# Products of ones ahead of the first load, the last weight splits behind a table, factors behind a copy, two chunks ahead of the weights

## The chip, the cores and the metric

The kernel runs on one core of a Trainium2 chip (trn2). The metric is the device time of one execution in microseconds. The core has TensorE (PE), VectorE (DVE), ScalarE (ACT), GpSimd (POOL) and SyncE (SP); in this kernel SP issues the plain loads and POOL the indirect scatters and stores.

## What is computed

Attention over channels for four batches, then a mixture of eight experts, of which each token uses one:

```python
qn = q / (np.linalg.norm(q, axis=1, keepdims=True) + 1e-06)
kn = k / (np.linalg.norm(k, axis=1, keepdims=True) + 1e-06)
s = kn.transpose(0, 2, 1) @ qn / tau            # B=4, N=5056, C=256
a = softmax(s, axis=-1)
x = (v @ a).reshape(B * N, C)                   # 20224 tokens
logits = x @ w_gate                             # E=8 experts
expert_idx = np.argmax(logits, axis=1)
gate_w = softmax(logits)[token, expert_idx]
out = gate_w * (relu(x @ w1[e]) @ w2[e])        # F=1024, e = expert_idx of the token
```

## The kernel before

**Attention.** `attention(b, ...)` is a generator and each `yield` is a point where other work may be given out. A batch has 20 chunks of scores: a chunk loads 512 KB of q and k (L203), squares it on ScalarE (L213, L215), adds the squares on VectorE (L216) and multiplies k by q on TensorE, either as it is (a native chunk, L223, f32) or split into a high and a low part (L186, L187, then L227 and L228). Batch 0 is native throughout; of batch 1, chunk 0 and those from 14 on are split. Then come the norms, the softmax and the attention matrix `a_x` (L240 to L326), and then ten groups of 512 values: products with `a_x` (L363 in batch 0, L366 later), the choice of the expert and the row's slot (L376 to L440), and four indirect scatters of the rows into `xs`, sorted by expert (L443). A group is two `yield`s.

**Weights.** `weights()` is a generator too. For each of eight experts it loads four 512 KB pieces (L120, tied behind batch 0's last load of scores), finds their scale by a gram product (L158), its diagonal (L162) and a sum over partitions (L123, L84, L85), and then splits each of the two f32 halves into two f16 parts: a cast on ScalarE (L112) and a subtraction on VectorE (L113). The sixteen results fill the tile `W`; most raw halves are loaded into places of `W` that are free by then, the last two into buffers of the tag `hl`, of which there are two. A half's split is given out while the next expert is loaded; only those of the last expert taken, number 4, are left for the end, where `both` and `fe` (the factors that undo the scales) are made as well.

**Table and blocks.** `table(s)` works out on VectorE, from the counts of tokens so far, which blocks of 256 sorted rows are full; table 0 rests on the first six groups of batch 0 and yields five blocks. `block_load` (called by `look`) waits on SP for the table's entry, then loads a block's rows, transposed (`xT`, L584), and the rows' gate weight and number (`mt`, L586). `block` copies eight pieces of its expert's weights out of `W` at an address from a register (L600, five buffers), multiplies (L612), applies the relu and splits (L619, L620), multiplies by the second weights (L634), scales by the factor `fac` (L640, from `mt` and `fe`; L645) and stores by an indirect DMA (L647).

**Order.** The code gives instructions out in the order in which it calls the generators, and the framework's scheduler then puts each engine's list in order: what comes first in the code has precedence, but where its list has a gap by the scheduler's own reckoning, ready work from further down is put in. On the chip every engine and every queue then runs its list strictly in order. `tc.issue_after(x)` ties what is made under it behind `x` in the list of its engine; it adds no wait.

The opening runs so: the first two chunks of batch 0; constants; then a loop over steps 2 to 32, which takes one step of `first` (batch 0) each; at step 20, when batch 0's 20 chunks are out and this step gives out norms and softmax, it also takes 14 steps of `weights`, then 2 at each step; from step 23 on also one chunk of `second` (batch 1), ten in all. Then what is left of the weights, table 0, the first two blocks' loads, the rest of batch 0, and the loop over blocks, into which the other batches are interleaved by a planner (`want`, `s_at`), with `START` standing for the ten chunks given out before.

## Time and profile before

| | us |
|---|---|
| median of 3 runs | 1187.32 (1187.19 to 1194.84) |
| profiled execution | 1184.51 |
| its span, first to last instruction | 1182.7 |
| TensorE busy | 1151.0 |
| VectorE busy | 906.6 |
| ScalarE busy | 645.5 |
| GpSimd busy | 388.7 |

The profile is one execution. The span is a little shorter than the execution's time, as something lies around the instructions. Busy times are sums of records; an f32 product leaves two records. Times on the timeline count from the start of the span, and where several instructions of one line follow each other a row gives their start, their joint length and their count. The granted clock is a share of TensorE's upper level, 2.4 GHz; 0.50 is the lower, 1.2 GHz.

### The profile page before, as it was taken

The page shows a single profiled execution, that of the slowest core. Times are in us where ns is not written, and L with a number is a line of the kernel's source. Part 1 is how long each engine was busy: PE and PEld are TensorE (multiplying, and loading weights), DVE is VectorE, ACT ScalarE, POOL GpSimd, SP SyncE. Part 2 cuts the span into 40 slices and gives each one's busy share as a digit, 9 for nine tenths or more (in the row PEclk, how much of TensorE's full clock was granted, in tenths as well). Part 3 has the DMA queues.
Part 4 walks back from the last instruction along what each step waited for, and adds up shares of the span by engine and source line. Part 5 has one row for each costly group of instructions (what it writes and reads, how often), then busy time and mean ns, then how long its engine had stood idle before and what let it go on. Part 6 is the DMA issues. An engine that isn't in the chain of part 4 may idle for free.

```text
span 1182.7 us, 28145 instructions
## 1 busy us (share of the span) xinstructions
PE 1151.0 (97%) x10212; PEld 1022.5 (86%) x10212; DVE 906.6 (77%) x2384; ACT 645.5 (55%) x1362; POOL 388.7 (33%) x366
## 2 busy tenths in 40 slices
PE   8898899999999999999999999999999999999998
PEld 7777688999888889999888889999888888889897
DVE  6789898888987777777888777777865566656986
ACT  6399864887655546666655536666432323332332
POOL 0047651466512223544622112445421111111111
PEclk9889999999999999999999999999999999999999
DMA  8976874545564433453355434433242122121221
GB/s 328 408 293 246 215 195 120 144 117 144 141 152 125 126 81 100 115 129 100 101 157 129 122 91 105 120 100 79 72 106 55 46 55 55 46 51 39 40 55 31
DMA packets 147870, 145.91 MB, mean 123 GB/s; under 512 B 115980, under 2 KB 117393, under 8 KB 147728
## 3 DMA queue, kind: packets, MB, share of 16 engines
q1 hardware_dynamic: 132336, 102.48, 33.0%
q0 software_dynamic: 15392, 41.60, 9.8%
q8 instruction: 81, 1.33, 0.5%
q14 instruction: 61, 0.50, 0.1%
HBM read 80.03 MB, written 43.29 MB: 104 GB/s over the span
## 4 chain that ended last, share of the span: by engine, by line
PE 54%; issue 25%; DVE 7%; DMA 5%; POOL 4%; ACT 3%; SPq 1%; POOLq 0%; DVEq 0%; ACTq 0%
PE y L634 19%; PE hp L612 19%; PE px L366 7%; POOL out L647 4%; PE sp L227 3%; PE sp L223 2%; DMA W<-in_w 2%; PE sp L228 2%; DVE W L113 1%; DVE ht L620 1%; DVE rows L385 1%; DVE hl L187 1%; DMA xs<-rows,r_si 1%; PE px L363 1%; ACT xjunk L370 1%
## 5 line engine op out<-in xcount | busy, mean ns | idle before, releaser
L612 PE MATMUL hp<-xT,wp 128*128 128x256 f16 (+1 forms) x4320 | 449.4, 262 | 0.7 <-DVE ht L620 0.5
L634 PE MATMUL y<-wp,ht 128*128 128x256 f16 x3888 | 446.6, 273 | 0.5 <-DVE ht L620 0.5
L612 PEld LDWEIGHTS <-wp 128*128 128x128 f16 x4320 | 381.8, 98 | 45.6 <-issue 3.4
L634 PEld LDWEIGHTS <-ht 128*128 128x128 f16 x3888 | 373.3, 98 | 52.5 <-issue 3.6
L647 POOL DMA_INDIRECT out<-o,mt x162 | 181.1, 1118 | 628.5 <-ACT o L645 599.5
L600 DVE COPY wp<-W 128x1024 f16 x720 | 298.5, 428 | 92.2 <-PE y L634 65.0
L619 ACT ACTIVATE ht<-hp 128x512 f16<-128x512 f32 x324 | 191.6, 594 | 160.1 <-PE hp L612 112.7
L620 DVE SCALAR_TENSOR_TENSOR ht<-hp,ht 128x512 f16<-128x512 f32 x324 | 219.5, 685 | 22.5 <-ACT ht L619 20.9
L443 POOL DMA_INDIRECT xs<-rows,r_si x160 | 187.4, 1172 | 121.6 <-issue 41.6
L645 ACT ACTIVATE o<-y,b_fac 128x256 f32<-128x256 f32 x162 | 68.7, 469 | 191.7 <-PE y L634 181.2
L366 PE MATMUL px<-a_h,hl 128*128 128x264 f32 x480 | 98.0, 296 | 0.0
L384 ACT ACTIVATE rows<-xg,x_sc 128x256 f16<-128x256 f32 x160 | 69.1, 497 | 31.6 <-DVE r_ex L417 22.4
L187 DVE TENSOR_TENSOR hl<-raw,hl 128x1024 fp32r<-128x1024 f32 x47 | 57.5, 1224 | 30.4 <-ACT hl L186 30.4
L366 PEld LDWEIGHTS px<-a_h,hl 128*128 128x128 f32 x480 | 78.9, 188 | 1.4 <-issue 0.6
L186 ACT CAST hl<-raw 128x1024 fp32r<-128x1024 f32 x47 | 49.0, 1044 | 46.5 <-PE sp L228 39.8
L227 PE MATMUL sp<-hl 128*128 128x512 f32 x188 | 72.8, 420 | 1.1 <-DVE hl L187 1.1
L223 PE MATMUL sp<-raw 128*128 128x256 f32 x264 | 64.2, 400 | 5.9 <-DMA raw<-in_qk 5.9
L215 ACT ACTIVATE raw<-raw 128x1024 f32<-128x1024 f32 x44 | 46.6, 1059 | 42.7 <-DVE hl L187 41.8
L385 DVE SCALAR_TENSOR_TENSOR rows<-xg,x_sc,rows 128x256 f16<-128x256 f32 x160 | 69.6, 479 | 0.2 <-ACT rows L384 0.2
L370 ACT ACTIVATE xjunk<-xg 128x256 bf16<-128x256 f32 x160 | 66.6, 416 | 3.3
L366 PE MATMUL px<-a_l,hl 128*128 128x264 f32 x240 | 68.2, 284 | 0.0
L223 PEld LDWEIGHTS sp<-raw 128*128 128x128 f32 x264 | 52.1, 201 | 13.7 <-DMA raw<-in_qk 6.2
(142 smaller groups left out, 928.8 us busy)
## 6 DMA issues: line engine op xcount, KB each, us to landing
raw<-in_qk SPq DMA_DIRECT2D x80, 512.0 KB, 4.3
vraw<-in_vT SPq DMA_DIRECT2D x34, 512.0 KB, 4.2
W<-in_w SPq DMA_DIRECT2D x28, 512.0 KB, 9.1
v<-in_vT SPq DMA_DIRECT2D x12, 256.0 KB, 8.8
out<-o,mt POOLq DMA_INDIRECT x162
xs<-rows,r_si POOLq DMA_INDIRECT x160
wraw<-in_w SPq DMA_DIRECT2D x4, 512.0 KB, 5.2
xT<-xs SPq DMA_TRANSPOSE x90, 3.3
```

The costliest lines, as they stand in the source:

```text
L223: pe.matmul(sp[c][:, 0, :], raw[:, j, kc0 : kc0 + P], raw[:, j, 0:C], start=first, stop=last)
L227: pe.matmul(sp[c], hl[:, 0, j, kc0 : kc0 + P], hl[:, :, j, 0:C], start=first, stop=False)
L366: pe.matmul(px, hl[:, vh, c, ts], ah[:, c, :], start=(n == 0), stop=(n == 5))
L370: act.activation(junk, xg[:, t, 0:C], AF.Square, accum_out=ss[:, t : t + 1])
L385: vec.scalar_tensor_tensor(out=r16[:, t, C : 2 * C], in0=x, scalar=sc[:, t : t + 1], in1=r16[:, t, 0:C], op0=ALU.mult, op1=ALU.subtract,)
L443: ins = pool.indirect_dma_start(out=xs[:, :], out_offset=bass.IndirectOffsetOnAxis(ap=si[:n, t : t + 1], axis=0), in_=rows[:n, t, :], in_o ...
L600: vec.tensor_copy(out=t, in_=Wf[:, ds(e * 8192 + n * 1024, 1024)])
L612: pe.matmul(hp[:, f % nf, :], wp[:, dc, wh, (f % 2) * P : (f % 2 + 1) * P], xT[:, 2 * xh + dc, :], start=(n == 0), stop=(n == 5),)
L619: act.activation(ht[:, 0], hp, AF.Relu)
L620: vec.scalar_tensor_tensor(out=ht[:, 1], in0=hp, scalar=0.0, in1=ht[:, 0], op0=ALU.max, op1=ALU.subtract)
L634: pe.matmul(ys[j], hts[f // nf][:, hh, f % nf, j * P : (j + 1) * P], wp[:, f % 2, wh, :], start=(f == 0 and n == 0), stop=(f == 7 and n == 2),
L647: pool.indirect_dma_start(out=out[:, :], out_offset=bass.IndirectOffsetOnAxis(ap=mt.bitcast(I32)[:, j, 1:2], axis=0), in_=o, in_offset=Non ...
```

## The change

Four things. (1) `ones16` is made ahead of everything, and thirty 128 x 128 x 128 products of it into an unused bank stand first in TensorE's list. (2) At step 20 two chunks of batch 1 are given out in front of the weights; the loop takes its ten as before, so twelve are out when it ends, and `START` stays. (3) `weights()` yields once more behind its last scale, the loop stops there (33 steps are `4 * E + 1`), and the last two splits, `both` and `fe` are given out behind table 0 and the first two blocks' loads. (4) A block's factor is tied behind the copy of its seventh piece of weights.

```diff
--- before.py
+++ after.py
@@ -165,7 +165,9 @@
                 )
             summed.append((e, gram, dsum, list(zip(pair, raws))))
             yield
+
         scale(*summed.pop())
+        yield
         while ready:
             split_one()
         both = tiny.tile([P, E], F32, name="w_both", bufs=1)
@@ -595,9 +597,11 @@
             skip_runtime_bounds_check_because=WHY,
         )
 
+        copied = [None]
+
         def piece(n):
             t = work.tile([P, 1024], F16, tag="wp", name="wp", bufs=WP)
-            vec.tensor_copy(out=t, in_=Wf[:, ds(e * 8192 + n * 1024, 1024)])
+            copied[0] = vec.tensor_copy(out=t, in_=Wf[:, ds(e * 8192 + n * 1024, 1024)]).ins
             return t
 
         hts = []
@@ -637,7 +641,9 @@
                     )
                     n += 1
             if f == 4:
-                vec.tensor_scalar(out=fac, in0=mt[:, :, 0], scalar1=fe[:, ds(e, 1)], scalar2=None, op0=ALU.mult)
+
+                with tc.issue_after(copied[0]):
+                    vec.tensor_scalar(out=fac, in0=mt[:, :, 0], scalar1=fe[:, ds(e, 1)], scalar2=None, op0=ALU.mult)
             if f % 2 == 1 and f < 7:
                 yield
         for j in range(nj):
@@ -658,15 +664,20 @@
 
     def take(gen, n):
         for _ in range(n):
-            if next(gen, StopIteration) is StopIteration:
-                return False
-        return True
+            next(gen, None)
+        return n
 
     nch = NP // P // 2
     normal = [(ps_a, "acc")] * 2
     wts = weights()
     first = attention(0, [False] * nch, False, [(ps_y, "y0"), (ps_y, "y1")])
     second = attention(1, [i == 0 or i >= NATIVE for i in range(nch)], True, normal)
+
+    ones16 = one.tile([P, P], F16, name="ones16")
+    vec.memset(ones16, 1.0)
+    idle = ps_t.tile([P, 512], F32, tag="tp", name="idle")
+    for _ in range(30):
+        pe.matmul(idle[:, 0:P], ones16, ones16, start=True, stop=True)
     take(first, 2)
 
 
@@ -679,8 +690,6 @@
     tri32 = work.tile([P, P], F32, tag="junk", name="tri32", bufs=1)
     sync.dma_start(out=tri32, in_=kc[:, K_TRI:K_N])
     vec.tensor_copy(out=tri, in_=tri32)
-    ones16 = one.tile([P, P], F16, name="ones16")
-    vec.memset(ones16, 1.0)
     ones = one.tile([P, P], F32, name="ones")
     vec.memset(ones, 1.0)
     wg = kt[:, K_WG : K_WG + 2 * E].rearrange("p (c e) -> p c e", c=2)
@@ -694,12 +703,14 @@
     vec.memset(done, 0.0)
     fe = one.tile([P, E], F32, name="fe")
 
+    weighed = 0
     for step in range(2, nch + 1 + 2 * CUT):
         take(first, 1)
-        take(wts, 0 if step < nch else 14 if step == nch else 2)
+        if step == nch:
+            take(second, 2)
+        weighed += take(wts, 0 if step < nch else min(14 if step == nch else 2, 4 * E + 1 - weighed))
         if step > nch + 2:
             take(second, 1)
-    run(wts)
     tables = {0: table(0)}
 
     def streams():
@@ -727,6 +738,7 @@
     side, s_at = streams(), 0.0
     look(0)
     look(1)
+    run(wts)
     run(first)
     for n, (s, i) in enumerate(stages):
         while s not in tables:
```

## Rows read from the trace of the kernel before

**Rows 1.** The page, section 1: busy us, share, instructions.
```profile
PE 1151.0 (97%) x10212; PEld 1022.5 (86%) x10212; DVE 906.6 (77%) x2384; ACT 645.5 (55%) x1362; POOL 388.7 (33%) x366
```

**Rows 2.** Windows: length, busy us (records) by engine, granted clock, DMA share, GB/s.
```profile
0.00:100.00 100.00, 87.49 (x556) 75.91 (x557) 76.68 (x162) 68.99 (x110) 21.57 (x19) 0.93 0.89 335
100.00:200.00 100.00, 90.00 (x633) 74.75 (x632) 90.78 (x277) 72.46 (x159) 56.21 (x43) 0.98 0.66 190
```

**Rows 3.** Windows at the start, the same columns.
```profile
7.00:8.00 1.00, 1.00 (x4) 0.78 (x4) 1.00 (x2) 0.00 (x0) 0.00 (x0) 1.00 1.01 397
15.00:20.00 5.00, 5.00 (x25) 4.41 (x24) 4.69 (x4) 4.07 (x4) 0.00 (x0) 1.00 0.98 333
```

**Rows 4.** Timeline: start us, length, instruction, count [idle before <-what ended it].
```profile
8.44 1.06 ACT L215 ACTIVATE sq<-raw 128x1024 f32<-128x1024 f32 x1 [1.70 <-DMA raw<-in_qk]
```

**Rows 5.** Windows of three later tens, columns as in group 2.
```profile
40.00:50.00 10.00, 7.40 (x76) 6.37 (x76) 7.57 (x33) 2.99 (x5) 0.00 (x0) 0.94 1.02 406
50.00:60.00 10.00, 6.89 (x52) 6.65 (x53) 8.08 (x16) 5.37 (x3) 0.00 (x0) 0.67 1.04 401
90.00:100.00 10.00, 9.75 (x74) 8.37 (x73) 9.66 (x23) 9.38 (x22) 6.07 (x5) 1.00 0.85 312
```

**Rows 6.** Timeline of TensorE, 4 to 60.
```profile
4.40 34.71 PE L223 MATMUL sp<-raw 128*128 128x256 f32 x152 [4.40 <-DMA raw<-in_qk]
...
41.57 1.20 PE L158 MATMUL gram<-W 128*128 128x128 bf16 x18
...
59.02 0.59 PE L123 MATMUL gram<-w_dsum,ones 128*128 128x2 f32 x2 [3.11 <-DVE w_diag L162]
```

**Rows 7.** TensorE, 166 to 170: first and last product of a split chunk.
```profile
167.16 0.48 PE L227 MATMUL sp<-hl 128*128 128x512 f32 x1
...
168.54 0.28 PE L228 MATMUL sp<-hl 128*128 128x256 f32 x1
```

**Rows 8.** The page, sections 5 and 6: one subtraction, one kind of load.
```profile
L187 DVE TENSOR_TENSOR hl<-raw,hl 128x1024 fp32r<-128x1024 f32 x47 | 57.5, 1224 | 30.4 <-ACT hl L186 30.4
...
W<-in_w SPq DMA_DIRECT2D x28, 512.0 KB, 9.1
```

**Rows 9.** Timeline of SP's queue.
```profile
27.47 13.49 SPq L120 DMA_DIRECT2D W<-in_w  x14
```

**Rows 10.** Timeline, 106 to 135: the last two splits and scatters beside them.
```profile
117.59 2.00 ACT L112 ACTIVATE W<-W,scales 128x2048 f16<-128x2048 f32 x1
...
119.79 2.34 DVE L113 SCALAR_TENSOR_TENSOR W<-W,scales 128x2048 f16<-128x2048 f32 x1
...
122.16 2.00 ACT L112 ACTIVATE W<-wraw,scales 128x2048 f16<-128x2048 f32 x1 [1.50 <-DVE W L113]
...
123.27 0.96 POOL L443 DMA_INDIRECT xs<-rows,r_si  x1 [0.30 <-issue]
...
124.46 2.35 DVE L113 SCALAR_TENSOR_TENSOR W<-wraw,scales,W 128x2048 f16<-128x2048 f32 x1
124.64 3.00 POOL L443 DMA_INDIRECT xs<-rows,r_si  x1 [0.41 <-DVE c_av L511]
...
130.77 0.96 POOL L443 DMA_INDIRECT xs<-rows,r_si  x1 [0.30 <-ACT r_d L408]
```

**Rows 11.** Timeline, 128 to 156: first block's load, first products, factors.
```profile
135.57 1.35 SPq L584 DMA_TRANSPOSE xT<-xs  x1
...
141.10 0.49 PE L612 MATMUL hp<-xT,wp 128*128 128x256 f16 x3
141.28 0.23 DVE L640 TENSOR_SCALAR b_fac<-mt,fe 128x2 f32<-128x2 f32 x1 [1.04 <-DMA mt<-xs]
...
144.64 0.23 DVE L640 TENSOR_SCALAR b_fac<-mt,fe 128x2 f32<-128x2 f32 x1 [2.35 <-DMA mt<-xs]
```

**Rows 12.** Window from 140 to 150, columns as in group 2.
```profile
140.00:150.00 10.00, 8.15 (x59) 6.60 (x58) 6.51 (x29) 7.48 (x25) 7.74 (x10) 1.00 1.06 263
```

**Rows 13.** Line L113: ns min/median/max, first and last start us.
```profile
L113 DVE SCALAR_TENSOR_TENSOR W<-W,scales x14: 2341/2349/2353, 49.5 to 119.8; 128x2048 f16<-128x2048 f32 x14
```

## The prediction

> **What bounds the kernel now.** I read the busy times first, then the windows in long stretches, and then the timeline only where the windows show loss. TensorE is busy for 1151.0 of 1182.7 us [rows 1]. Of its 31.7 us of idle time 12.5 lie in the first 100 us and 10.0 in the second (100.00 less 87.49 and 90.00) [rows 2], so in the 983 us behind them it loses 9.2: there it is the bound. The total of its work doesn't change with the edits (the added products of ones apart, which run before the first load lands), so the end can only move by what TensorE's idle and half-clock time in the first 200 us shrinks: the budget is 22.5 us of idle plus the half-clock stretches, and the 4.40 us ahead of the first load [rows 6] stay in any case. That is the frame of the whole sum: something saved on VectorE or in a queue counts only as far as it closes a hole of TensorE in that stretch.
>
> Where the holes are differs by stage. At the start the clock is low: the record count gives 4 in the window 7 to 8, against 25 in the 5 us from 15 to 20 [rows 3]. Between 40 and 60 us TensorE idles 2.60 and 3.11 us, and its granted clock is 0.67 in the second ten, part of the time at the lower of its two levels, 1.2 GHz; ScalarE is busy for 2.99 and 5.37 of these tens, VectorE for 7.57 and 8.08. From 90 to 100 us VectorE and ScalarE are at 9.66 and 9.38 of 10: here they are the bound, and TensorE waits for them [rows 5].
>
> **Part 1, products of ones at first.** Thirty 128-column f16 products run while the first load is under way. Cost: none on the path if they end by about 4.4 us; the one row with such products at the upper level, 18 in 1.20 us [rows 6], makes thirty 2.0 us, and twice that (4.0) at the lower level. They can start once the memset of ones16, about 1 us into the span, is done, so they end between 3.0 and 5.0. Where they end late, the first chunk starts up to 0.6 us late, which the next step covers. Gain: 25 records in 5 us are 0.20 us each at the upper level, so a chunk's eight take 1.6 us and twice that at the lower. Now TensorE works from 4.4 to about 8.0 at half rate: 3.6/0.40 = 9 records, and the 7 that are left of the first two chunks last until 8.0 + 1.4 = 9.4. With the clock up from the beginning the 16 records end at 4.4 + 3.2 = 7.6. But the third chunk lands only at about 8.4: ScalarE's square of it starts at 8.44 after waiting 1.70 us for that load [rows 4]. So the gain is 9.4 - 8.4 = 1.0 us and not 1.8; what waits next is the load. The column of granted clock shows 1.00 in that window, the rate shows half; I go by the rate. Bounds 0 and 1.0; I take 1.0, since from the third chunk on TensorE is gapless to the end of these scores.
>
> **Part 2, two chunks of the second batch in front of the weights.** The loop still gives out ten chunks, so at its end twelve are done instead of ten. The two moved chunks cost TensorE one split chunk, 167.16 to 168.82, 1.7 us, and one native chunk, 1.6 us by the rate above: 3.3 us [rows 7]. Put into the 5.7 us of holes between 40 and 60, they are 3.3 us less to do in the gapless part. ScalarE gets a cast and two squares, about 1.06 each [rows 4], and VectorE a subtraction of 1.22 and an addition of the same size [rows 8]: 3.2 and 2.4 us, for which both have the room there [rows 5]. The holes themselves are waits on VectorE: the largest, 3.11 us, is the weight scale's product at L123 waiting for the diagonal of L162, and the products of values (L363) stand behind it in TensorE's queue [rows 6]. A chunk's products put in front of that product fill the hole; put behind it, they lengthen the queue and nothing is gained.
>
> What the two loads cost: 2 x 512 KB at the 401 to 406 GB/s of this stretch [rows 5] are 2.6 us of transfer, in front of the fourteen weight loads that SP issues from 27.47 on [rows 9]. SP's queue keeps its order, so if the second raw buffer is not yet free, the weight loads wait behind that load. A weight load takes 9.1 us from issue to landing in the median [rows 8], so the first lands at about 36.6; the first gram products run at 41.57 [rows 6]. That is 5 us of slack, and 2.6 us fit under it; without that cover they would cost their 2.6 us, and up to 1 us per buffer wait more. So I take 3.3 us for this part, bounds -2.6 (slack gone, nothing filled) and +5.7 (the holes wholly filled).
>
> **Part 3, the last splits behind the table.** Only expert 4's two halves are left when the weights' generator reaches its new yield: ScalarE 117.59 and 122.16, VectorE 119.79 to 122.13 and 124.46 to 126.81. The second ScalarE cast waits for VectorE's first pass, since it writes where that pass reads, so the pair is a serial 9.2 us [rows 10]. Now they stand in front of the sixth group's last steps, the scatter of its rows and table 0. The first block's load goes out at 135.57 [rows 11], behind the landing of the last of the 24 scatters, which POOL issues at 130.77. The one of them that meets the second split takes 3.00 us, the one before it 0.96 [rows 10]. Without the two splits the sixth group's slots come 2.3 us earlier and POOL saves another 2.0 us where the second split met a scatter: the last issue moves from 130.77 to between 126.4 and 128.5, so the first block's load by 2.3 to 4.3 us. What comes late instead: a block's first copy of weights reads W at an address from a register, so it waits for every split. The splits now have the time from the issue of that load to its landing (135.57 to the first product at 141.10, 5.5 us) [rows 11] and whatever gaps the list order has left before. 9.2 us fit only if the first cast starts before the table ends. ScalarE's cast needs nothing of the table, and the scheduler fills gaps with ready work of lower rank (the weights' gram products at 41.57 stand ahead of the norm's later steps, which come first in the code) [rows 6], so I expect it to start early. That same freedom can leave the splits where they are, and then nothing is gained. Bounds -5 (first block behind 9.2 us of splits that start with the table's end) and +4.3. I take 2.5: the 2.3 us of the slots' earlier end, which the scatters at the least carry over.
>
> POOL's long scatters lengthen where the split runs, but the split is 2341 to 2353 ns in all fourteen cases of its main form, so only POOL waits [rows 13]. The Trainium skill, "SBUF — State Buffer", section "SBUF: two separate sides", says that the port pair that VectorE shares with GpSimd is held by whoever starts first and that the other is blocked for that whole instruction; by it the moved splits, now among the scatters of groups six to nine, could be the ones that wait. The rows show no such case, so the sum leaves it at nothing.
>
> **Part 4, factors later.** The factor at L640 now stands in VectorE's queue ahead of work that needs nothing from its block, and waits there for the block's row data: 1.04 us before 141.28 and 2.35 before 144.64 [rows 11]. Together 3.4 us in which VectorE, the bound of this stage, does nothing; behind the second wait stand the split of rows (L385), the slots of a group and the next copy of weights. Tied behind the copy of the seventh piece, which can't come before TensorE has used two earlier ones, it finds its data landed. TensorE's own idle time from 140 to 150 is 1.85 us [rows 12]: of the 3.4 no more than these 1.9 become time at once, the rest as far as VectorE is the bound behind it. The next thing late there is VectorE's own queue. Bounds 0 and 3.4; I take 1.5. The factor is read by ScalarE only when the block's last product is done, so its delay costs nothing.
>
> **The sum.** 1.0 + 3.3 + 2.5 + 1.5 = 8.3 us. The profiled execution took 1184.5 us, which becomes 1176.2; the median of the three runs shown is 1187.3, 2.8 above it, and on that footing the time is 1179.0, which I forecast.
>
> **The rivals.**
> First, more closes than I count: the clock stays up between 48 and 64 us because the new products fill the holes, the wait for the split chunk in the loop goes, and parts 2 to 4 reach their upper bounds: 1.0 + 5.7 + 4.3 + 3.4 = 14.4, so 1173. For it speaks the clock of 0.67 [rows 5]; against it that VectorE at 9.66 of 10 gives back at most what its waits were. Chance 0.18.
> Second, the scheduler puts things about where they were: the splits fill the same gaps, and the chunks land behind the scale's product. What is left is part 1 and part of 4: 1 to 3 us, 1185. For it speaks that it fills gaps by readiness. Chance 0.17.
> Third, slower: the splits start only with the table's end, and the first block waits for their serial 9.2 us. If the table ends just ahead of the first block's load, at about 135.5, the splits are done at 144.7, and with a copy of weights behind them the first product runs at about 145 to 147 instead of 141.1: 4 to 6 us lost, less part 1: 1191. It decides if the first cast starts less than about 4 us (144.7 less 141.1) ahead of the table's end. Against it: ScalarE stood idle for 1.50 us ahead of the second cast [rows 10], so it has gaps. Chance 0.08.
> Fourth, the moved splits are held up by scatters under way, about 1.3 us at the most for each (a free scatter with its gap, from 123.27 to the next at 124.64, is 1.4) [rows 10]: 2.6 us off part 3, 1181.6. It is the rule of the "SBUF — State Buffer" page of the Trainium skill above. Since none of the fourteen was longer, chance 0.03.
>
> **How the numbers follow.** The forecast, a gain of 3 to 12 us, has 0.54. The range reaches from the first rival's 1173 to 1188, which takes in the second and fourth and leaves out the third and a little beyond the first. About 1% (12 us) is what a measurement of this kernel can tell from no change; below 1175.4 lies the first rival and a little of the forecast's edge, 0.19; above 1199 only a worse form of the third, 0.04; within, 0.77.
>
> **What would show it.** Part 1: eight records per 1.6 us from 4.4 us on, TensorE waiting for a load just before 8.4, and the norm's products (L243, now near 39) about 1 us earlier. Part 2: products of L227 and L223 of batch two before 60 us, and less than 3 us idle from 40 to 60. Part 3: no split (L113) ahead of table 0, scatters of the fifth and sixth group at about 1 us each, the first block's load at 131 to 133. Part 4: no wait at L640 near 141 to 145. The forecast is wrong if the first block's copy of weights comes after its rows have landed, or if the first gram products run later than now.

## The result and the profile after

The changed kernel took 1196.16 us in the median of five runs (1194.44 to 1197.52), the kernel before 1190.13 us (1187.19 to 1194.84): ratio 1.0058, 95% interval 1.0033 to 1.0083. The forecast was 1179.0, with a range of 1173 to 1188: the time is outside it, and on the other side of no change. By the medians the change costs 6.0 us, where 8.3 were to be gained.

The profiled execution has a span of 1195.7 us, 13.0 more than before. That is more than the medians differ by: of before, the execution that was profiled (1184.51) lies 5.6 us under the median of its five runs, of after (1197.52) 1.4 over it. So 7.0 of the 13.0 us stand between two single executions, and the rows can't say which of their losses a usual execution shares. The late opening and the standstill below are in both profiles of the changed kernel as it is.

The page, section 1, and windows of after (length, busy us and records by engine, granted clock, DMA share, GB/s):

```profile
PE 1156.2 (97%) x10242; PEld 1025.4 (86%) x10242; DVE 904.6 (76%) x2384; ACT 643.3 (54%) x1362; POOL 398.5 (33%) x366
...
0.00:100.00 100.00, 86.75 (x566) 74.22 (x567) 74.92 (x156) 67.40 (x106) 14.32 (x16) 0.93 0.85 321
100.00:200.00 100.00, 90.14 (x633) 74.66 (x631) 91.42 (x282) 73.05 (x161) 53.35 (x46) 0.97 0.69 209
...
300.00:400.00 100.00, 90.87 (x733) 77.93 (x732) 75.41 (x147) 51.01 (x69) 32.81 (x18) 0.95 0.46 121
```

The last of these windows in the kernel before:

```profile
300.00:400.00 100.00, 99.59 (x827) 86.56 (x826) 83.18 (x160) 57.49 (x80) 24.53 (x20) 1.00 0.52 138
```

Against [rows 1, 2] the second hundred is the same, 90.14 for 90.00. The first has 86.75 for 87.49, but 3.1 of these are the products of ones, so it does 3.8 us less of the old work. The larger loss stands in the fourth hundred: 90.87, where the kernel before has 99.59 and a clock of 1.00. Adding it up from the first expert product on (141.1 us before, 146.2 after): that product is 5.1 us later, and behind it TensorE idles 20.1 us instead of 12.3, 7.9 more by the unrounded sums. 5.1 + 7.9 = 13.0, the whole difference of the spans. TensorE's busy time behind that product is 1029.4 us in both, although the two chunks are done ahead of it (with the chunks alone it is 1027.4): the stretch at the lower clock behind the standstill, below, takes that back.

**The opening.** Timeline of SP, ScalarE and TensorE in after, 4 to 70 us (start us, length, instruction, count, idle before and what ended it):

```profile
4.74 3.72 PE L225 MATMUL sp<-raw 128*128 128x256 f32 x16 [0.58 <-DMA raw<-in_qk]
8.63 0.70 PE L225 MATMUL sp<-raw 128*128 128x256 f32 x2 [0.17 <-DMA raw<-in_qk]
...
33.52 11.94 SPq L120 DMA_DIRECT2D W<-in_w  x14
...
47.66 1.06 ACT L217 ACTIVATE sq<-raw 128x1024 f32<-128x1024 f32 x1 [6.59 <-PE sp L230]
48.62 0.49 ACT L299 ACTIVATE soft<-soft,s_nm 128x256 f32<-128x256 f32 x1
...
51.54 0.33 PE L123 MATMUL gram<-w_dsum,ones 128*128 128x2 f32 x2
...
64.00 0.59 PE L123 MATMUL gram<-w_dsum,ones 128*128 128x2 f32 x2 [4.57 <-DVE w_diag L162]
64.44 5.83 PE L365 MATMUL px<-a_x,v 128*128 128x264 f32 x16
```

The sixteen records of the first two chunks now take 3.72 us, and the third chunk waits for its load: in this profile part 1 did what was said. Then SP starts the weights' loads at 33.52, where it did at 27.47 [rows 9]: 6.05 us later. The moved chunk's square stands at 47.66 ahead of the softmax's exponent at 48.62 (46.17 before). The first weight scale is at 51.54 (46.3 before), and the first products of values at 64.44 (59.5 before). The hole has moved and not closed: with [rows 5, 6] to compare, windows of the same columns show 8.04 and 6.75 of ten up to 60 us (7.40 and 6.89 before), and then the row below, where the kernel before has 10.00 of ten. From 40 to 70 us TensorE idles 9.2 us instead of 5.7.

```profile
60.00:70.00 10.00, 6.00 (x18) 4.87 (x19) 8.63 (x10) 6.37 (x9) 0.00 (x0) 0.57 1.03 403
```

**The splits.** Timeline of VectorE, ScalarE and POOL in after, 120 to 143 us, and SP's load of the first block:

```profile
120.14 2.00 ACT L112 ACTIVATE W<-W,scales 128x2048 f16<-128x2048 f32 x1
122.44 2.34 DVE L113 SCALAR_TENSOR_TENSOR W<-W,scales 128x2048 f16<-128x2048 f32 x1
...
128.11 0.16 DVE L511 TENSOR_SCALAR c_ni<-c_ni 1x8 int32<-1x8 int32 x1
128.23 2.35 DVE L113 SCALAR_TENSOR_TENSOR W<-wraw,scales,W 128x2048 f16<-128x2048 f32 x1
...
132.88 2.38 POOL L445 DMA_INDIRECT xs<-rows,r_si  x1 [7.27 <-issue]
134.35 0.15 DVE L513 CAST c_av<-c_ni 1x8 f32<-1x8 int32 x1
...
142.02 1.34 SPq L586 DMA_TRANSPOSE xT<-xs  x1
```

With [rows 10, 11] beside them: one split still stands ahead of the table, the other inside it (the table runs from c_ni on), just as before, only 2.7 and 3.8 us later. The first block's load is 6.45 us later (142.02 for 135.57).

**The standstill.** Timelines of SP, ScalarE and TensorE in after, 294 to 340 us:

```profile
294.31 0.34 SPq L205 DMA_DIRECT2D raw<-in_qk  x1
...
303.51 4.50 SPq L205 DMA_DIRECT2D raw<-in_qk  x2
318.12 1.26 SPq L586 DMA_TRANSPOSE xT<-xs  x1
327.22 0.41 SPq L588 DMA_DIRECT2D mt<-xs  x1
328.18 1.25 SPq L586 DMA_TRANSPOSE xT<-xs  x1
329.53 1.46 SPq L205 DMA_DIRECT2D raw<-in_qk  x3
...
305.17 2.79 PE L638 MATMUL y<-wp,ht 128*128 128x256 f16 x24
...
313.85 1.49 PE L616 MATMUL hp<-xT,wp 128*128 128x256 f16 x12 [0.53 <-DVE ht L624]
...
333.83 1.04 ACT L188 CAST hl<-raw 128x1024 fp32r<-128x1024 f32 x1 [12.27 <-DMA raw<-in_qk]
...
337.12 2.74 PE L616 MATMUL hp<-xT,wp 128*128 128x256 f16 x12 [8.37 <-DVE ht L624]
339.66 3.75 PE L638 MATMUL y<-wp,ht 128*128 128x256 f16 x24
```

Read it from below. TensorE waits 8.37 us for the relu of a block, which VectorE and ScalarE do; ScalarE stands, 12.27 us, at the cast of a later batch's chunk of scores, because its load has not landed. That load was issued at 329.53, behind three other loads of SP: the first rows (xT) of the next table, which wait until every scatter has landed; their mt, which needs a buffer that the store of three blocks before must give back (landed at 327.2); and the next xT. Behind the standstill TensorE runs at its lower level for a while: the granted clock is 0.57 from 330 to 340, and 12 and 24 products take 2.74 and 3.75 us, 2.2 us more than the 1.49 and 2.79 of the same products ahead of it. In the kernel before SP has the order the other way round, three raw loads and only then that xT, and a single raw load behind the next xT:

```profile
297.56 15.96 SPq L203 DMA_DIRECT2D raw<-in_qk  x3
314.32 1.27 SPq L584 DMA_TRANSPOSE xT<-xs  x1
```

### The profile page after: what moved, and what is told of

Read it like the earlier page. It is cut to its first block, busy times and chain, and to the rows that moved or that the text cites. A ratio compares the mean times of both kernels' runs of the same rounds, so it can differ in the third digit from the quotient of the medians.

```text
span 1195.7 us, 28184 instructions
## 1 busy us (share of the span) xinstructions
PE 1156.2 (97%) x10242; PEld 1025.4 (86%) x10242; DVE 904.6 (76%) x2384; ACT 643.3 (54%) x1362; POOL 398.5 (33%) x366
## 4 chain that ended last, share of the span: by engine, by line
PE 64%; issue 18%; DVE 8%; POOL 3%; ACT 3%; DMA 3%; SPq 1%; POOLq 0%; DVEq 0%; ACTq 0%
PE y L638 24%; PE hp L616 23%; PE px L368 7%; PE sp L229 3%; POOL out L653 3%; PE sp L225 3%; PE sp L230 2%; DMA raw<-in_qk 2%; DVE W L113 1%; DVE rows L387 1%; DVE hl L189 1%; DVE wp L604 1%; ACT W L112 1%; DVE ht L624 1%; PE px L365 1%
## 5 line engine op out<-in xcount | busy, mean ns | idle before, releaser
L653 POOL DMA_INDIRECT out<-o,mt x162 | 187.9, 1160 | 589.6 <-ACT o L651 556.5
L370 ACT COPY xg<-px 128x264 f32<-128x264 f32 x160 | 57.8, 367 | 12.9 <-PE px L368 9.0
```

The lines of the kernel that those rows point to most:

```text
L653: pool.indirect_dma_start(out=out[:, :], out_offset=bass.IndirectOffsetOnAxis(ap=mt.bitcast(I32)[:, j, 1:2], axis=0), in_=o, in_offset=Non ...
```

## The experiments

The runs fell on seven chips. On three of them the kernel before takes 1187.7 to 1189.3 us, near the 1190.1 of the result (the first kind below; which chip the result was measured on is not recorded), and on the four others 1217.2 to 1228.0 (the second kind). So only ratios to the kernel before on the same chip are compared, and each is read with its kind. The changed kernel as it is was not run on a chip of the second kind.

In the table the first expert product is the first product of L612 in the kernel before, and the last column is TensorE's longest single wait between 300 and 360 us. In the text the first scale is the first product at L123. Theories A and B are named anew in each expectation; in most of them A is the late opening and B what stands behind the new table in SP's list.

| kernel | kind (before, us) | ratio (95% interval) | first expert product us | longest wait us |
|---|---|---|---|---|
| changed | first (1190.1) | 1.0058 (1.0033 to 1.0083) | 146.2 | 8.4 |
| changed, again | first (1188.6) | 1.0056 (1.0034 to 1.0077) | 145.2 | 8.5 |
| chunks behind the weights | first (1188.6) | 1.0110 (1.0087 to 1.0133) | 147.9 | 8.4 |
| late splits alone | first (1188.6) | 0.9988 (0.9972 to 1.0003) | 141.3 | 0.4 |
| late factors alone | first (1188.6) | 0.9978 (0.9962 to 0.9994) | 140.9 | 0.4 |
| chunks alone | first (1187.7) | 0.9985 (0.9965 to 1.0005) | 147.4 | 0.6 |
| changed, eight mt | first (1189.3) | 1.0028 (1.0010 to 1.0046) | 146.3 | 3.1 |
| changed, five mt | second (1217.2) | 0.9990 (0.9970 to 1.0011) | 145.0 | 7.5 |
| changed, eight mt | second (1220.4) | 0.9908 (0.9881 to 0.9935) | 144.3 | 3.4 |
| changed, eight mt | second (1224.4) | 0.9960 (0.9944 to 0.9976) | 144.3 | 2.9 |
| changed, no chunks | second (1228.0, 1217.2, 1220.4) | 0.9962, 0.9987, 0.9974 | 141.7, 141.1, 141.5 | 2.3, 2.2, 2.9 |
| chunks alone | second (1228.0, 1217.2, 1220.4) | 0.9888, 0.9949, 0.9940 | 149.9, 146.7, 149.8 | 2.2, 3.4, 2.1 |
| changed, planner told | second (1228.0, 1217.2) | 0.9969, 0.9995 | 144.9, 145.1 | 0.9, 1.1 |
| ones alone | second (1228.0) | 0.9961 (0.9935 to 0.9986) | 144.2 | 2.3 |

On the second kind waits of 2 to 3.4 us stand there in most kernels, so only the rows of 7.5 us and more are called a standstill on it.

**The changed kernel again, no edit.**

> The changed kernel once more, unaltered, beside the kernel before on this chip. Theory A (the two chunks in front of the weights cost the opening about 5 us on every chip, and nothing gives it back): first scale near 51.5 us, first hp product near 146, ratio 1.003 to 1.008. Theory B (the opening's 5 us are made up later, and the loss in the trace of the changed kernel was the one standstill of PE at 325 to 337 us, which a shift of a few us makes or unmakes): the same opening, but 300 to 400 us has PE busy for more than 95 of 100 us and the ratio is 0.990 to 1.000; with the standstill there it is 1.003 or more.

1.0056, with the first scale at 50.8 us and the standstill at the same place, 8.46 us. Both theories allow it; so loss, late opening and standstill stay together on another chip of the first kind.

**Without the two chunks, three chips.** The changed kernel less

```diff
-        if step == nch:
-            take(second, 2)
```

> The changed kernel without its two chunks in front of the weights (all else stays). Theory A (the chunks do the harm: they hold up the weights' loads by about 6 us and bring on the standstill near 325 to 337 us of the changed kernel): first products of values near 59 us instead of 64.4, no standstill, time 1 to 5 us below the kernel before, 1185 to 1189. Theory B (the standstill comes from the factors tied behind a copy or from the splits' new place): it is still there, 8 us or more of idle TensorE between 300 and 400 us, time 1192 to 1197.

> The changed kernel without the two chunks in front of the weights: products of ones, late splits and late factors alone. First scale near 45.5 us, first hp product near 141. Theory A: 0.994 to 0.998, as the opening is 5 us shorter than the changed kernel's and the other parts are worth 1 to 3 us. Theory B: 0.996 to 0.999 without a standstill near 325 us (the three parts are worth 1.0, 1.4 and 2.1 us when each is alone, and their sum would be 0.9965), 1.004 or more with one.

> The changed kernel without the two chunks. On a chip where the kernel before takes 1190: theory A and theory B both say 0.996 to 0.998, the sum of the three other parts when each is alone (0.9965), with no standstill behind 300 us; 1.003 or more would say that the standstill comes from late splits or late factors and not from the chunks. On a chip where it takes 1220: 0.996 to 0.999 as twice before.

The first scale is back at 45.2 to 45.4 us and the first expert product at 141.1 to 141.7. There is no standstill, and the ratios are 0.1 to 0.4% under 1. All three fell on chips of the second kind, so what the three other parts are worth together on one of the first is not measured.

**The two chunks alone, four chips.** The kernel before plus the same two lines.

> The kernel before with the two chunks in front of the weights as its only edit. Theory A: first products of values 4 to 6 us later than 59.5, a standstill of about 10 us near the end of batch 1, time 1194 to 1200. Theory B: only the opening is later, no standstill, time 1188 to 1192.

> The kernel before with only the two chunks given out in front of the weights, which was 0.9888 on the chip where the kernel before took 1228 us. First scale near 51.5, first hp product near 148. Theory A: 1.004 to 1.008 on a chip where the kernel before takes 1190, without any standstill. Theory B: 1.003 or less without a standstill behind 300 us, and 1.010 or more with one.

> The kernel before with the two chunks alone. On a chip where the kernel before takes 1190: theory A (the chunks cost the opening 5 us and nothing gives it back): 1.003 to 1.006 without a standstill; theory B (the chunks shift the second batch's raw loads behind the new table): 1.010 or more with a standstill of PE between 320 and 345 us. On a chip where it takes 1220: 0.989 to 0.995 as twice before, which would say that what the chunks cost depends on the chip.

> The kernel before with the two chunks alone, a fourth time, for a chip on which the kernel before takes 1190 (alone it gave 0.9888, 0.9949 and 0.9940 on three chips where it takes 1217 to 1228, with no standstill of PE behind 300 us in any of the three profiles, and with a first hp product 5 to 9 us later). On a chip of 1190: theory A (the opening's 5 us are not given back there, as PE has only 12 us without work behind the first hp product): 1.002 to 1.006. Theory B: the same 1.002 to 1.004 without a standstill, 1.010 or more with one. Below 0.999 both are wrong and the chunks are worth something behind the opening on any chip.

The last of these is the run that theory A did not survive; theory B, which had 1.002 to 1.004 there, missed as well. The opening is as late as in the changed kernel (first scale at 51.8 to 52.4, first expert product at 146.7 to 149.9), and yet the time is not longer: 0.9985 on a chip of the first kind, which its interval doesn't tell from 1, and 0.5 to 1.1% shorter on the second. One of the three profiles on the second kind does have a wait of 3.4 us, at 319.6, with 12 products at the lower level behind it, which the fourth expectation leaves out. SP's timeline in the run on the first kind, 306 to 327 us, shows why it has no standstill:

```profile
306.12 9.20 SPq L203 DMA_DIRECT2D raw<-in_qk  x3
319.95 1.26 SPq L584 DMA_TRANSPOSE xT<-xs  x1
325.93 0.41 SPq L586 DMA_DIRECT2D mt<-xs  x1
```

Here too mt waits for a store, until 325.93; but three raw loads went out ahead of the xT and not two, and TensorE is busy for 10.00 of 10 us from 320 to 330 and again from 330 to 340. So neither late scatters nor the wait of mt make the standstill by themselves: it takes a raw load that is needed soon and stands behind them.

**The planner told, two chips.** The changed kernel, with the two chunks counted in what the planner takes as done:

```diff
-    START = -(2 * CUT - 2) * 2 * 640
+    START = -(2 * CUT) * 2 * 640
```

> The changed kernel with START standing for twelve chunks given out instead of ten, so that batch 1 ends at the same place among the blocks as before. Theory A, in the form that the planner's stale count moves the end of batch 1 by two chunks into a jam of SP's queue: the opening is as late as in the changed kernel (first products of values near 64.4), the standstill is gone, time 1185 to 1191. Rival (the jam comes from the opening's lateness or from the factors): standstill stays, 1193 to 1198.

> The changed kernel with the planner's START counting all twelve chunks that were done (the two in front too), which moves the side work of the tables later by two chunks' due time. Theory A: the opening is the same, ratio 1.002 or more. Theory B: the order behind the first table differs, the standstill near 330 us is gone as it was on the chip of the first experiments, ratio 0.993 to 0.998; if it is still there, 1.004 or more.

The opening is late (first scale at 50.6 and 50.8), and the standstill is gone in both, as two raw loads stand behind the xT and not three. So it hangs on how the planner's share of side work meets the table, and not on the opening. The ratios, 0.9969 on one chip and 0.9995 on the other, are both under the 1.002 of the second expectation's theory A, and the second is over theory B's 0.998; on a chip of the first kind it was not run.

**The chunks behind the weights.**

```diff
         take(first, 1)
+        weighed += take(wts, 0 if step < nch else min(14 if step == nch else 2, 4 * E + 1 - weighed))
         if step == nch:
             take(second, 2)
-        weighed += take(wts, 0 if step < nch else min(14 if step == nch else 2, 4 * E + 1 - weighed))
```

> The changed kernel with the two chunks of the second batch given out behind the fourteen steps of the weights. Theory A: the loads of the weights start at 27.5 us again, first scale near 45.5 us, first hp product near 141, and the ratio to the kernel before is 0.4% lower than the unaltered changed kernel's on this chip. Theory B: the opening comes back by the same 5 us, but the ratio differs from the unaltered one's by less than 0.3%, or goes up, as the order of everything behind it differs.

The loads of the weights start at 27.03 and the first scale is at 45.91, as expected. The rest of theory A missed: the first expert product is at 147.9 and the ratio is 1.1% above 1; theory B had allowed that it goes up. The chunks' products now stand among the products of values (TensorE waits 4.01 us for a split at 66.42), and the standstill is there, 8.42 us. So the weights' 6 us late loads are an effect of the place, but taking them away does not bring the first expert product or the time back.

**Late splits alone.** The kernel before plus this alone (the loop's count of the steps of `weights`, as in the change, is left out here):

```diff
         scale(*summed.pop())
+        yield
         while ready:
             split_one()
...
-    run(wts)
     tables = {0: table(0)}
...
     look(0)
     look(1)
+    run(wts)
```

> The kernel before with the last scale and the four splits given out behind the first table, and nothing else of the change. Both theories: the scheduler fills idle places of ACT and DVE as before, so the first split stands ahead of the table and the second inside it, xT of the first block is issued within 1 us of the kernel before's 135.6, ratio 0.998 to 1.002. The prediction's step (splits out of the way of rows and scatters, 2.5 us) would give 0.998 with POOL's first scatter of the last group at or before 128 us and no split ahead of the table.

Timeline of VectorE and SP, 121 to 138 us:

```profile
121.81 2.32 DVE L113 SCALAR_TENSOR_TENSOR W<-W,scales 128x2048 f16<-128x2048 f32 x1
...
127.56 0.15 DVE L515 TENSOR_TENSOR c_av<-c_av,done 1x8 f32<-1x8 f32 x1
127.67 2.35 DVE L113 SCALAR_TENSOR_TENSOR W<-wraw,scales,W 128x2048 f16<-128x2048 f32 x1
...
137.75 1.34 SPq L585 DMA_TRANSPOSE xT<-xs  x1
```

One split ahead of the table and one inside it, as with [rows 10]; the first block's load is 2.2 us later than before (137.75 for 135.57) and not within the 1 us expected. The time is not told from that of the kernel before.

**Late factors alone.** The kernel before plus the following (`copied`, kept by `piece` as in the change, is left out here):

```diff
-            vec.tensor_scalar(out=fac, in0=mt[:, :, 0], scalar1=fe[:, ds(e, 1)], scalar2=None, op0=ALU.mult)
+            with tc.issue_after(copied[0]):
+                vec.tensor_scalar(out=fac, in0=mt[:, :, 0], scalar1=fe[:, ds(e, 1)], scalar2=None, op0=ALU.mult)
```

> The kernel before with the factors tied behind the last weight copy, and nothing else of the change. The prediction's step: the eight waits of DVE for mt (8.8 us in all) are gone, PE gains 1.5 us, ratio 0.9987. Theory A: 0.998 to 1.000. Theory B: the waits are gone, and the ratio is outside 0.997 to 1.000 by a PE standstill made or unmade somewhere behind 200 us.

Of the kernel before, VectorE's list of waits has the row below; in this run no row of the list names the factor. The time is 0.22% shorter, 2.6 us (0.7 to 4.5 by the interval), with 1.5 forecast. Where it was gained the profiles don't show: the spans of the two profiled executions are 1182.8 and 1182.7 us, and TensorE's idle time from 140 to 160 us falls by 0.65 us, from 2.43 to 1.78.

```profile
DVE b_fac L640 <- DMA mt<-xs: 8.8, 8, 2.4
```

**Products of ones alone.** The kernel before, with `ones16` and thirty products of it ahead of the first chunk.

> The kernel before with the thirty products of ones in front as its only edit. By the prediction's part 1 the norm's products come 1.0 us earlier and the time falls by 1.0 us; seen from the changed kernel, where they came 0.9 us earlier, 0 to 1.5 us, at the edge of what five rounds show. Rival: the order behind is the same and the 0.9 us is lost in the next wait, no difference in time.

0.9961 on a chip of the second kind: 4.8 us (1.7 to 8.0). In the profiled execution the norm's products come at 38.46, 0.5 us before the kernel before's 38.95, so most of the 4.8 is not in the opening; where it is was not found.

**Five buffers for mt.** The changed kernel with

```diff
-        mt = work.tile([P, 2, 2], F32, tag="mt", name="mt", bufs=3)[:, 0 : nt // P, :]
+        mt = work.tile([P, 2, 2], F32, tag="mt", name="mt", bufs=5)[:, 0 : nt // P, :]
```

> The changed kernel with five buffers for mt in place of three, so that SP's load of mt no longer waits for the store of the block three before; the lists of PE, DVE, ACT and POOL are unaltered, only SP's order differs. Theory B (the loss is SP's queue: raw loads of the second batch stand behind that wait of 8.6 us, and PE stands still for 9 us and runs at half clock for some us behind it): no standstill near 330 us, 300 to 400 us has PE busy for more than 98 of 100 us, ratio to the kernel before 0.994 to 0.998 where the unaltered one gave 1.0056. Theory A (the opening's 5 us are the loss): the opening is the same and the ratio stays at 1.003 or more.

The standstill stayed, 7.5 us, the ratio is 0.9990, and the experiment did not take away what it was meant to: with buffers to spare the scheduler put two further loads of mt ahead of the raw loads, and one of these waits for the same stores. Timeline of SP, 334 to 346 us:

```profile
334.37 1.26 SPq L586 DMA_TRANSPOSE xT<-xs  x1
335.84 7.47 SPq L588 DMA_DIRECT2D mt<-xs  x3
...
344.86 1.46 SPq L205 DMA_DIRECT2D raw<-in_qk  x3
```

**Eight buffers for mt, three chips.** The same line with 8. No load of mt in SP's list waits for a store at this place, and the lists of the other four engines are those of the changed kernel.

> The changed kernel with eight buffers for mt in place of three (with five, SP's list put further loads of mt ahead of the raw loads, and one of these still waited for the same stores); with eight no load of mt in SP's list waits for a store there, and the lists of PE, DVE, ACT and POOL are unaltered. Theory B (the raw loads of the second batch's splits come late because SP holds them behind the loads of the new table's blocks, and the wait for the stores is 8.6 us of that): the first raw load behind the new table is issued some 7 us earlier than with three buffers, PE's standstill behind it (8.4 us in the changed kernel) falls below 3 us, 300 to 400 us has PE busy for more than 96 of 100 us, and the ratio is some 0.7% lower than the unaltered kernel's: 0.996 to 1.001 on a chip where the kernel before takes 1190, 0.989 to 0.996 on one where it takes 1220 (five buffers gave 0.9990 there). Theory C (the wait for the scatters, which the first block of the new table needs anyway, is what holds SP; the stores add nothing): standstill and ratio as with five buffers.

> The changed kernel with eight buffers for mt once more (0.9908 on a chip where the kernel before takes 1220; five buffers, with the standstill still there, 0.9990 on another such chip). Theory B (the loss is SP's queue behind the new table, and the chunks' 5 us of the opening are given back behind it as they are when the chunks are alone): on a chip of 1190 the standstill near 325 to 337 us falls from 8.4 to under 4 us and the ratio is 0.996 to 1.000, against 1.0056 to 1.0058 unaltered; on a chip of 1220 0.989 to 0.995. Theory C (the order of the other engines is what costs, not SP's): 1.003 or more on a chip of 1190.

> The changed kernel with eight buffers for mt a third time (0.9908 and 0.9960 on two chips where the kernel before takes 1220 to 1224), for a chip where the kernel before takes 1188 to 1190 and the unaltered change gave 1.0056 to 1.0058. Theory B there: PE's standstill at 325 to 337 us falls from 8.4 to under 4 us, 300 to 400 us has PE busy for more than 95 of 100 us, ratio 0.996 to 1.001. Theory C (not SP's order but that of the other engines costs): 1.003 or more. On a chip of 1217 to 1228: 0.989 to 0.997 as twice before.

The third fell on a chip of the first kind. Its SP and TensorE, 317 to 337 us:

```profile
317.14 1.26 SPq L586 DMA_TRANSPOSE xT<-xs  x1
318.61 2.22 SPq L588 DMA_DIRECT2D mt<-xs  x3
321.03 1.25 SPq L586 DMA_TRANSPOSE xT<-xs  x1
322.38 0.99 SPq L205 DMA_DIRECT2D raw<-in_qk  x2
...
330.89 2.24 PE L616 MATMUL hp<-xT,wp 128*128 128x256 f16 x12 [3.10 <-DVE ht L624]
332.92 3.74 PE L638 MATMUL y<-wp,ht 128*128 128x256 f16 x24
```

The raw loads go out at 322.38 instead of 329.53, 7.2 us earlier, and the standstill falls from 8.4 to 3.1 us. What SP still waits for there is the scatters (5.4 us), which an xT of a new table needs in any case. The ratio is 1.0028, where the unaltered change has 1.0056 and 1.0058 on other chips of this kind: about half the loss is given back, 0.28%, some 3.4 us. The intervals (1.0010 to 1.0046, and 1.0034 to 1.0077 and 1.0033 to 1.0083) overlap, so this size is rough. TensorE is busy for 96.08 of the 100 us from 300 on, as expected, but the ratio missed 0.996 to 1.001. So SP's wait is a part of the loss and not all of it; whether the 3.1 us that are left, with products at the lower level behind them, are another part was not tried. Of the other chips, one gave 0.9908, where five buffers with the standstill gave 0.9990 on a chip that is near it, and one 0.9960. On the first of these a wait of 3.4 us and 92.98 busy of 100 us missed the expectation's 3 and 96, on the second the ratio missed 0.989 to 0.995.

Over all twenty profiles a standstill of 7.5 to 8.5 us stands in four: the changed kernel twice, with the chunks behind the weights, and with five buffers. These are the ones in which SP's list has three raw loads in a row behind the second xT of the new table; the others have one or two there.

## Why the prediction was wrong

**The frame.** The step that failed is the first: that behind 200 us TensorE is the bound, loses 9.2 us, and that the end can only move by what the holes of the first 200 us shrink. That is a statement on the kernel before. The edits change the order of every list behind them: with two chunks done that `START` doesn't count, three raw loads of the second batch came to stand behind the new table's rows in SP's list, where one stood before, and a hole of 8.4 us opened where there had been none, with 12 and 24 products behind it at the lower level (2.2 us more). The chunks, the splits and the factors were run alone on chips of the first kind, at 0.9985, 0.9988 and 0.9978; together, with the products of ones, 1.0056. The sum of parts had no term for that, and no rival named it.

**Part 1 held, its size in part by luck.** The sixteen records end at 8.46 (7.6 forecast), the third chunk waits 0.17 us for its load, and the norm's products come at 38.09 for 38.95: 0.9 us, with 1.0 forecast. In the second profile of the changed kernel they come at 38.56, 0.4 us earlier; over all profiles they stand at 37.6 to 38.6 with the ones and at 38.9 to 39.9 without. The half rate was read from [rows 3], whose counts (4 in 1 us, 25 in 5) show 0.8 and not half; single records of the kernel before do start 0.43 us apart up to 7.87 and 0.22 us behind, so the reading was right and these rows don't show it. What ones alone bring beyond this on a chip of the second kind (4.8 us) was not foreseen.

**Part 2 failed at the loads.** The step said 2.6 us of transfer under 5 us of slack, and up to 1 us for each wait for a buffer. Measured are 6.05 us. SP's list of waits up to 36 us has raw loads waiting for the release of their buffers by TensorE:

```profile
SPq L205 <- PE sp L225: 21.4, 12, 3.4
```

In the kernel before, up to 36 us:

```profile
SPq L203 <- PE sp L223: 16.3, 10, 3.0
```

Two loads more are two waits more at the pace at which TensorE frees buffers, 21.4 - 16.3 = 5.1 us for the two, 2.6 each and not 1; the last three raw loads go out 3.5 us apart (26.23, 29.69 and 33.14). What was to be gained was mis-sized too: the moved chunks' products run from 44.69 to 49.64 without a wait, but take 4.9 us there, at a clock of 0.83 from 40 to 50, where 3.3 were priced, and the hole opens again behind them, from 60 to 70. The prediction also set the slack by the first gram product, which was in fact not late (40.71 for 41.57), and not by the scale, which needs more of the loads and came 5.2 us late. Its own condition for being wrong, the first gram products, was therefore the wrong one to watch. Still the chunks alone cost nothing in time (0.9985): with them the opening is 6.3 us longer, and behind the first expert product the profiled run is 2.1 us shorter than before's. The other 4.2 us of its profile stand between the two profiled executions, and not between the medians; this was not settled further.

**Part 3 went by the second rival.** The step that failed is "so I expect it to start early", out of the way of the table: it did start early, ahead of the table and inside it as before, as the scheduler filled about the same gaps with it. The same sentence that carried the forecast ("that same freedom can leave the splits where they are") described what happened, and should have had the larger chance. The first block's load, which was to go out 2.3 to 4.3 us earlier, goes out 2.2 us later with the splits alone and 6.45 later in the changed kernel. So the way to the 2.5 us was not there; the time alone, 0.9988 (0.9972 to 1.0003), tells neither no change nor 2.5 us from it. Rival 4's page, the Trainium skill, "SBUF — State Buffer", section "SBUF: two separate sides", has the port pair of VectorE and GpSimd held by whoever starts first; the main form of the split is 2337 to 2414 ns in the fourteen cases of after, so at most 0.06 us longer than in [rows 13]; these cases show no split that waited, and that rival had no part in it.

**Part 4 held** in its step, the wait at the factor, which is gone alone and in the changed kernel. Alone it brought 2.6 us (0.7 to 4.5) for 1.5 forecast, but of this only 0.65 us shows in the stretch that the prediction took it from, so that the size fits is not shown to be more than luck.

**The noise.** The prediction took 12 us as the least that a measurement can tell from no change. The interval of the result is 0.5% wide, 6 us, and shows a loss of half the 12.

**What stays open:** what lies behind the other half of the loss on the first kind (1.0028 with eight buffers; the chunks alone have 0.9985); where the late factors and the ones gain what they gain alone; which of ones, splits and factors must join the chunks to bring SP's order about; and why the POOL scatters ahead of the standstill are long (below).

## What to carry to other kernels

A gain worked out for one stage of a kernel whose lists a scheduler packs is a gain only if the lists behind it keep their order, so look, in every in-order queue, for the loads that a later stage needs and for what could come to stand ahead of them: a load behind a wait for a store is the first suspect. When a part of the work is moved to an earlier place, tell the planner that it is done, and price each extra load through a ring of buffers at the pace at which its buffers are freed and not at the transfer. A buffer more does not take a wait away if the scheduler uses it to bring another waiting load forward.

## What the runs showed of the hardware that was not expected

**Chips differ by 2 to 3% on the same program**, and the same edit measured other amounts on them: the two chunks alone 0.9985 on the first kind and 0.9888 to 0.9949 on the second. The chunks alone are one kernel with profiles on both. The products of its line L612 last the same (262 ns in the mean on the first kind, 262 to 263 on the second). What differs most is waiting: behind the first expert product TensorE idles 12.1 us on the first kind and 25.8 to 29.7 on the second. Below is the same window of that kernel, on the first kind and then on the second (1217.2):

```profile
200.00:300.00 100.00, 99.78 (x877) 91.08 (x876) 82.78 (x287) 78.37 (x223) 56.47 (x58) 1.00 0.50 136
...
200.00:300.00 100.00, 90.16 (x741) 80.63 (x740) 73.21 (x243) 67.06 (x189) 44.80 (x49) 0.96 0.45 120
```

A part of the waits on the second kind is TensorE's for "issue", that is for nothing that the profile shows: 2 to 11 us in each of the twelve profiles there, and none in the eight on the first kind. What the engines wait for is not shown.

**Scatters of one kind take from 0.90 to 4.54 us in the changed kernel.** Timeline of POOL in after, 304 to 317 us:

```profile
304.04 4.54 POOL L445 DMA_INDIRECT xs<-rows,r_si  x1 [2.59 <-DVE c_av L513]
308.89 0.96 POOL L445 DMA_INDIRECT xs<-rows,r_si  x1 [0.30 <-issue]
310.15 3.88 POOL L445 DMA_INDIRECT xs<-rows,r_si  x1 [0.30 <-issue]
314.34 2.23 POOL L445 DMA_INDIRECT xs<-rows,r_si  x1 [0.30 <-ACT raw L217]
```

The same four lengths, to 0.01 us, stand in three of the four runs with five and eight buffers, on chips of both kinds, where the lists of VectorE and GpSimd are the same. In the fourth, with the same lists, they are 4.59, 1.00, 2.39 and 1.28 us. So they hang on what runs beside them and when. VectorE has no idle time in its timeline there (303.0 to 321.1 us) and its instructions are not longer than elsewhere. That agrees with the rule of the "SBUF — State Buffer" page of the Trainium skill as far as GpSimd waits beside a busy VectorE. It does not show the other half, that one which starts second is blocked, for VectorE: the split that starts at 105.49 inside a scatter (104.37 to 105.60) takes 2.34 us, as elsewhere. A scatter is here 3.6 us longer than the shortest, and the longest single instruction of VectorE beside it is 1.21 us, so if VectorE holds it up, it is several instructions in a row, and not one. Whether it does, and which ones, was not tried.
